# Top-k attention and a low-rank mixer on one core: a transfer queue in program order, and both heads of a pair's third step transposed by VectorE and transfers

## The chip, the core and the metric

The kernel runs on one core of a Trainium2 chip. The core has five engines that each work through their own list of instructions in order: TensorE (PE in the profile, with PEld for the loads of its stationary operand), VectorE (DVE), ScalarE (ACT), GpSimd (POOL) and SyncE (SP), which here does nothing but issue transfers. They meet through semaphores. The metric is the time of one execution on the device in microseconds, from the first to the last instruction; the kernel before takes 1765.89 us in the median of three runs (1764.58 to 1766.87).

## The reference

For 8 batches of 8 heads with 576 rows and a head size of 64, each row of scores keeps its 32 largest entries, goes through a softmax and weighs the values; then a mixer and a two-layer network run over the result.

```python
scores = scale * np.matmul(q, k.transpose(0, 1, 3, 2))          # 8 x 8 x 576 x 576
kth = np.partition(scores, -32, axis=-1)[..., -32:-31]
scores = np.where(scores >= kth, scores, -1000000000.0)
attn = np.exp(scores - np.max(scores, axis=-1, keepdims=True))
attn = attn / (np.sum(attn, axis=-1, keepdims=True) + 1e-09)
x = np.matmul(attn, v)      # then (batch, row, head*64): 8 x 576 x 512
# mixer: U (576 x 32), V (32 x 576), w_ch1 (512 x 2048), w_ch2 (2048 x 512)
h = x.transpose(0, 2, 1) @ U @ V
u = x + h.transpose(0, 2, 1)
out = u + np.maximum(u @ w_ch1, 0.0) @ w_ch2
```

## The kernel before

Two heads are worked on together as a pair; there are 32 pairs, `g`, four to a batch. A pair has five steps: in steps `t` = 0 to 3, 128 rows of both heads; in step 4 the last 64 rows of both heads together, which makes it a short step. The steps of all pairs are counted by `n`, with `g, t = divmod(n, CH)` and `CH = 5`.

In each step VectorE finds the 32 largest of every row by four rounds of "eight largest" and "replace these eight" (lines 385, 396, 400). GpSimd and ScalarE mask the scores, and ScalarE takes the exponential into `E` (line 351). To multiply `E` by the values, TensorE needs it transposed. In the early pairs TensorE transposes both heads itself, by four 128x128 transposes for each head and one for the two 64-wide remainders, and ScalarE copies the result out of PSUM into `PT`. From pair 6 on (`shared`), only head 0 goes that way; head 1 is transposed in 32x32 blocks by VectorE into `y`, and the blocks are brought into order by transfers: four writes from `y` to a DRAM tile `away`, then one read from `away` into `PT`. All of these are issued by SyncE.

```python
    def shared(g, t):
        return t < NT and g * CH + t >= ROUNDED          # ROUNDED = 30: pairs 6 to 31, NT = 4

    def blocks(g, t):
        E2 = probs[g, t]
        PT = attn.tile([P, 2 * NT + 1, P], F32, tag="PT", name="PT")
        PTs[g, t] = PT
        y = attn.tile([P, 4, NT, BLK], F32, tag="y", name="y", bufs=1)
        nc.vector.transpose(                                            # line 447
            y.rearrange("p r c j -> p c r j"),
            E2[:, S + TAIL : 2 * S].rearrange("p (c r j) -> p c r j", c=NT, r=4),
        )
        away = dram.tile([P, 4, P], F32, tag="away", name="away")
        for a in range(4):
            nc.sync.dma_start(                                          # line 453
                away[:, a].rearrange("(r i) n -> i r n", r=4),
                y[a * BLK : (a + 1) * BLK].rearrange("i r c j -> i r (c j)"),
            )
        nc.sync.dma_start(                                              # line 457
            PT[:, NT : 2 * NT].rearrange("p a n -> p (a n)"), away.rearrange("p a n -> p (a n)")
        )

    def turns(g, t):
        ...
        for h in range(1 if shared(g, t) else nh):
            tp = ps_t.tile([P, NT, P], F32, tag="tp", name="tp")
            for j in range(NT):
                a = h * (S + TAIL) + j * P
                nc.tensor.transpose(tp[:, j, :], E2[:, a : a + P], ident)   # line 475
            nc.scalar.copy(PT[:, NT * h : NT * h + NT], tp)                 # line 476
            yield
        tp = ps_t.tile([P, P], F32, tag="tp", name="tp")
        ...
        nc.tensor.transpose(tp, E2[:, a : a + P], ident)                    # line 480
        nc.scalar.copy(PT[:, NT * nh], tp)                                  # line 481
        yield

    def values(g, t):
        ...
        nc.tensor.matmul(O, lhsT=vd, rhs=PT[:, 2 * NT], start=True, stop=False)   # line 509
        PB = PT[:, NT : 2 * NT].rearrange("p a (c j) -> p c a j", c=NT) if shared(g, t) else None
        for j in range(NT):
            for h in range(2):
                nc.tensor.matmul(                                           # line 513
                    O[half(h)],
                    lhsT=va[:, h, j, :],
                    rhs=PB[:, j] if h and shared(g, t) else PT[:, NT * h + j],
                    start=False,
                    stop=(j == NT - 1),
                )
        ...
        nc.scalar.copy(XTs[g][:, cols(t)], O)                               # line 522
```

The two-layer network of a batch (`mlp`, lines 582 and 601) is 4096 matmuls over the whole kernel's 8 batches, and is cut into small portions. A call of `fill()` puts the next portion into TensorE's list; how much is fixed by counts (`share`), not by time. The order of everything in a step from pair 4 on is written out by hand:

```python
        away = n <= STEPS and shared(*divmod(n - 1, CH))
        ...
        fill()
        next(turning, None)          # transposes of step n-1 on TensorE: turns(n-1)
        fill()
        next(turning, None)
        if away:
            next(last)               # exponential of head 1 of step n-1
        fill()
        next(turning, None)
        fill()
        if ease:
            next(last, None)         # exponential of head 0 of step n-1
        if n - 2 >= ALONE:
            values(*divmod(n - 2, CH))
        if n + 1 < STEPS:
            scores(*divmod(n + 1, CH))        # lines 333, and 320 for the short step
        next(here, None)             # a round of the top-k search of step n on VectorE
        next_params(1)
        ...
        fill()
        next(here, None)
        if away:
            blocks(*divmod(n - 1, CH))
        fill()
        if n <= STEPS:
            turning = turns(*divmod(n - 1, CH))
        fill()
        next(here, None)
        ...
        fill()
```

So the block transposes of step `n-1` are made in the middle of step `n`, and its values are multiplied in the middle of step `n+1`. At the top of step 0 of each pair `load(g + 1)` brings in the next pair's inputs: 21 transfers from pair 5 on. The output of the network leaves by `turned_back`, called from within `fill()`: a transpose on TensorE (line 649), a copy on ScalarE (line 651), one or two transfers (lines 655, 660).

Before, the order of TensorE, ScalarE, VectorE and GpSimd is that of the program (`manual_schedule`); the order of SyncE's transfers is chosen by the framework's scheduler:

```python
    HT = 10       # buffers of the network's hidden layer, two 320-wide slices each
    PE, ACT = mybir.EngineType.PE, mybir.EngineType.Activation
    DVE, POOL = mybir.EngineType.DVE, mybir.EngineType.Pool
    ...
    ctx.enter_context(tc.manual_schedule(engines={PE, ACT, DVE, POOL}))
```

Of the kernel before, what the change touches and what calls it, by code (L numbers as in the profile page):

```python
# [8 lines left out]
F32 = mybir.dt.float32  # L9
# [17 lines left out]
def kernel(  # L27
# [29 lines left out]
    B, H, S, D = q.shape  # L57
    P = 128
# [4 lines left out]
    NT, TAIL = 4, 64  # L63
    MAIN = NT * P
# [5 lines left out]
    CH = NT + 1  # L70
# [3 lines left out]
    NV = 3  # L74

    BLK = 32
    HT = 10
    PE, ACT = mybir.EngineType.PE, mybir.EngineType.Activation
    DVE, POOL = mybir.EngineType.DVE, mybir.EngineType.Pool

    const = ctx.enter_context(tc.tile_pool(name="const", bufs=1))
    loads = ctx.enter_context(tc.tile_pool(name="loads", bufs=1))
    attn = ctx.enter_context(tc.tile_pool(name="attn", bufs=2))
# [3 lines left out]
    ps_s = ctx.enter_context(tc.tile_pool(name="ps_s", bufs=2, space=bass.MemoryType.PSUM))  # L87
    ps_t = ctx.enter_context(tc.tile_pool(name="ps_t", bufs=2, space=bass.MemoryType.PSUM))
    ps_m = ctx.enter_context(tc.tile_pool(name="ps_m", bufs=2, space=bass.MemoryType.PSUM))
    ctx.enter_context(tc.manual_schedule(engines={PE, ACT, DVE, POOL}))  # L90


    PARTS = ((0, 1, NT), (2, 3))
# [141 lines left out]
    probs, PTs = {}, {}  # L235
# [199 lines left out]
    def shared(g, t):  # L435


        return t < NT and g * CH + t >= ROUNDED

    def blocks(g, t):  # L440


        E2 = probs[g, t]
        PT = attn.tile([P, 2 * NT + 1, P], F32, tag="PT", name="PT")
        PTs[g, t] = PT
        y = attn.tile([P, 4, NT, BLK], F32, tag="y", name="y", bufs=1)
        nc.vector.transpose(
            y.rearrange("p r c j -> p c r j"),
            E2[:, S + TAIL : 2 * S].rearrange("p (c r j) -> p c r j", c=NT, r=4),
        )  # L450
        away = dram.tile([P, 4, P], F32, tag="away", name="away")
        for a in range(4):
            nc.sync.dma_start(
                away[:, a].rearrange("(r i) n -> i r n", r=4),
                y[a * BLK : (a + 1) * BLK].rearrange("i r c j -> i r (c j)"),
            )
        nc.sync.dma_start(
            PT[:, NT : 2 * NT].rearrange("p a n -> p (a n)"), away.rearrange("p a n -> p (a n)")
        )

    def turns(g, t):


        E2 = probs.pop((g, t))
        nh = 2 if t < NT else 1
        if shared(g, t):
            PT = PTs[g, t]
        else:
            PT = attn.tile([P, 2 * NT + 1, P], F32, tag="PT", name="PT")
            PTs[g, t] = PT  # L470
        for h in range(1 if shared(g, t) else nh):
            tp = ps_t.tile([P, NT, P], F32, tag="tp", name="tp")
            for j in range(NT):
                a = h * (S + TAIL) + j * P
                nc.tensor.transpose(tp[:, j, :], E2[:, a : a + P], ident)  # L475
            nc.scalar.copy(PT[:, NT * h : NT * h + NT], tp)  # L476
            yield
        tp = ps_t.tile([P, P], F32, tag="tp", name="tp")
        a = MAIN if nh == 2 else S - P
        nc.tensor.transpose(tp, E2[:, a : a + P], ident)  # L480
        nc.scalar.copy(PT[:, NT * nh], tp)
        yield

    def inverse(g, lo, hi):
        den = dens[g][:, lo:hi]
        if g == NPAIR - 1:
            nc.vector.tensor_scalar_add(den, den, 1e-9)
        nc.vector.reciprocal(den, den)

    def values(g, t):  # L490

        PT = PTs.pop((g, t))
        va, vd, vt = (a[g % NV] for a in (vas, vds, vts))
        O = ps_t.tile([P, P], F32, tag="tp", name="O")
        if t == NT:
            den, x = dens[g], xs[g % 2]
            inverse(g, 2 * NT if g == NPAIR - 1 else 0, 2 * NT + 1)
            for j in range(NT + 1):
                nc.tensor.matmul(  # L499
                    O,  # L500
                    lhsT=PT[:, j],
                    rhs=va[:, :, j, :] if j < NT else vt,
                    start=(j == 0),
                    stop=(j == NT),
                )
            for h in range(2):
                nc.scalar.mul(x[half(h), NT, half(h)], O[half(h), half(h)], den[half(h), 2 * NT :])
            return
        nc.tensor.matmul(O, lhsT=vd, rhs=PT[:, 2 * NT], start=True, stop=False)  # L509
        PB = PT[:, NT : 2 * NT].rearrange("p a (c j) -> p c a j", c=NT) if shared(g, t) else None  # L510
        for j in range(NT):
            for h in range(2):
                nc.tensor.matmul(  # L513
                    O[half(h)],
                    lhsT=va[:, h, j, :],
                    rhs=PB[:, j] if h and shared(g, t) else PT[:, NT * h + j],
                    start=False,
                    stop=(j == NT - 1),
                )
        if t == 0:  # L520
            XTs[g] = attn.tile([P, MAIN], F32, tag="XT", name="XT")
        nc.scalar.copy(XTs[g][:, cols(t)], O)  # L522
# [49 lines left out]
    def mlp(b):  # L572
# [3 lines left out]
        for chunks, (lo, hi) in zip(PARTS, SPAN):  # L576
            w = hi - lo
            hTs = []
            for f in range(NF):
# [11 lines left out]
                if f % 2 == 0:  # L591
                    hT = mlpp.tile([P, 2, WIDE], F32, tag="hT", name="hT", bufs=HT)
                    hTs += [hT[:, 0], hT[:, 1]]
# [102 lines left out]
    t = 0  # L696
# [5 lines left out]
    for n in range(STEPS + 2):  # L702
        g, t = divmod(n, CH)
        if n < STEPS:
            if t == 0 and g + 1 < NP:
                load(g + 1)
            if t == 1 and g + 1 < NP:
                ready = prep(g + 1)
            fronts[n] = front(g, t)
            next(fronts[n])  # L710
        here, last = fronts.get(n, iter(())), fronts.pop(n - 1, iter(()))
        if n >= ALONE - 1 and n <= ALONE:

            if n < ALONE:
                next(last)
                values(*divmod(n - 3, CH))
                list(turning)
                next(here)
                next(last)
                scores(*divmod(n + 1, CH))  # L720
                values(*divmod(n - 2, CH))
            list(turns(*divmod(n - 1, CH)))
            values(*divmod(n - 1, CH))
            if n < ALONE:
                next(here)
                next(here)
                inverse(g, 0, 2 * NT)
                mixing.append(mixed(g, 1))
                fill()
                next(here)  # L730
                continue
            fill()
            scores(*divmod(n + 1, CH))
            next(here)
            while mixing:
# [3 lines that stand above are left out]
            next(last, None)  # L739
            next(here)  # L740
            fill()
            next(here)
            next(here)
            fill()
            continue
        ease = eased(*divmod(n - 1, CH))
        if n < ALONE:
            if ease:
                next(last, None)
            scores(*divmod(n + 1, CH))  # L750
            if n >= 3:
                values(*divmod(n - 3, CH))
                if (n - 3) % CH == NT:
                    mixing.append(mixed((n - 3) // CH, 3))
            list(turning)
            fill()
            next(here)
            if t < NT:
                next_params(1)
            fill()  # L760
            next(ready, None)
            next(here)
            next(last, None)
            fill()
            next(here)
            if t in (0, 1):
                next_params(1)
            next(here)
            fill()
            if n >= 1:  # L770
                turning = turns(*divmod(n - 1, CH))
            continue
        away = n <= STEPS and shared(*divmod(n - 1, CH))
        if ease:
            next(last, None)
# [5 lines that stand above are left out]
            next(last)  # L781
# [4 lines that stand above are left out]
            next(last, None)  # L786
# [3 lines that stand above are left out]
            scores(*divmod(n + 1, CH))  # L790
        next(here, None)
        next_params(1)
        if n - 2 >= ALONE and (n - 2) % CH == NT:
            mixing.append(mixed((n - 2) // CH, 5))
        fill()
        next(here, None)
        if away:
            blocks(*divmod(n - 1, CH))
        fill()
        if n <= STEPS:  # L800
            turning = turns(*divmod(n - 1, CH))
        fill()
        next(here, None)
        next(ready, None)
        if t in (1, 3):
# [3 lines that stand above are left out]
# [33 lines left out]
```

## Time and profile before

| | before |
|---|---|
| time, median of 3 | 1765.89 us |
| span of the profiled execution | 1765.1 us |
| TensorE busy, matmuls | 1670.0 us (95%) |
| weight loads busy | 1259.5 us (71%) |
| VectorE busy | 1540.3 us (87%) |
| ScalarE busy | 1026.2 us (58%) |
| GpSimd busy | 846.4 us (48%) |
| transfers on SyncE's queue | 110.68 MB, 26.0% of 16 engines' span |
| transposes of `E`, line 475 | 736 in 184 groups of four |
| block transposes, line 447 | 104 |

The profile gives each engine's busy time, then the same cut into 40 equal slices of 44.1 us, one digit each (9 means 90% or more). It follows back the chain of work that ended last, and lists groups of instructions with count, busy time, mean duration of one and the idle time before them. Besides this page there are answers of the trace: a table of busy times over chosen windows, and a timeline of each engine with start, length, line and, in brackets, the idle time before an instruction and what ended it. A run of equal instructions is one row of the timeline, so its length reaches from the start of the first to the end of the last.

### The profile page before, as it was taken

The page shows a single profiled execution, that of the slowest core. Times are in us where ns is not written, and L with a number is a line of the kernel's source. Part 1 is how long each engine was busy: PE and PEld are TensorE (multiplying, and loading weights), DVE is VectorE, ACT ScalarE, POOL GpSimd, SP SyncE. Part 2 cuts the span into 40 slices and gives each one's busy share as a digit, 9 for nine tenths or more (in the row PEclk, how much of TensorE's full clock was granted, in tenths as well). Part 3 has the DMA queues.
Part 4 walks back from the last instruction along what each step waited for, and adds up shares of the span by engine and source line. Part 5 has one row for each costly group of instructions (what it writes and reads, how often), then busy time and mean ns, then how long its engine had stood idle before and what let it go on. Part 6 is the DMA issues. An engine that isn't in the chain of part 4 may idle for free.

```text
span 1765.1 us, 28989 instructions
## 1 busy us (share of the span) xinstructions
PE 1670.0 (95%) x9851; PEld 1259.5 (71%) x9851; DVE 1540.3 (87%) x3106; ACT 1026.2 (58%) x2682; POOL 846.4 (48%) x591
## 2 busy tenths in 40 slices
PE   4576889999999999999999999999999999999999
PEld 2444556777777877788777877788777877788677
DVE  7999989999999999999999999999999999994000
ACT  4778787655655665565656556565656656564100
POOL 4777677445545454444444454545354554543000
PEclk7677799999999999999999999999999999999999
DMA  3232232232223332222223232223233232211010
GB/s 99 84 90 72 81 85 61 51 66 70 66 59 76 72 72 64 67 66 66 61 62 81 66 72 63 70 61 70 58 68 80 64 76 56 56 45 45 4 15 13
DMA packets 275829, 112.79 MB, mean 64 GB/s; under 512 B 173920, under 2 KB 260192, under 8 KB 275680
## 3 DMA queue, kind: packets, MB, share of 16 engines
q1 hardware_dynamic: 274624, 110.68, 26.0%
q8 instruction: 77, 1.26, 0.3%
q14 instruction: 72, 0.59, 0.1%
q10 hardware_dynamic: 1056, 0.26, 0.1%
HBM read 74.15 MB, written 36.70 MB: 63 GB/s over the span
## 4 chain that ended last, share of the span: by engine, by line
PE 78%; DVE 13%; POOL 4%; ACT 3%; issue 1%; DMA 1%; SPq 0%; POOLq 0%; DVEq 0%
PE mm L582 26%; PE mm L601 25%; PE sc L333 7%; PE O L513 6%; DVE rr L396 6%; DVE m L400 5%; PE tp L475 3%; DVE first L385 2%; PE sc L320 2%; PE O L499 2%; PE up L557 1%; PE O L509 1%; POOL E L403 1%; PE up L559 1%; PE tp L649 1%
## 5 line engine op out<-in xcount | busy, mean ns | idle before, releaser
L400 DVE MAX8 m<-rr 128x8 f32<-128x576 f32 x864 | 614.3, 747 | 5.5
L601 PE MATMUL mm<-hT,w 128*128 128x256 f32 (+1 forms) x2048 | 547.4, 410 | 0.0
L582 PE MATMUL mm<-uT,w 128*128 128x256 f32 (+1 forms) x2048 | 541.1, 410 | 0.8 <-ACT hT L594 0.8
L403 POOL TENSOR_SCALAR E<-Ssb,m 128x576 f32<-128x576 f32 x127 | 280.9, 2212 | 366.2 <-DVE m L400 346.1
L582 PEld LDWEIGHTS mm<-uT,w 128*128 128x128 f32 x2048 | 371.7, 190 | 114.7 <-issue 26.0
L601 PEld LDWEIGHTS mm<-hT,w 128*128 128x128 f32 x2048 | 368.5, 190 | 106.6 <-issue 22.5
L396 DVE MATCH_REPLACE8 rr<-m,rr 128x576 f32<-128x576 f32 x576 | 423.2, 741 | 0.0
L422 POOL TENSOR_TENSOR Ssb<-Ssb,E 128x576 f32<-128x576 f32 x159 | 224.8, 1414 | 147.6 <-ACT E L421 147.6
L594 ACT ACTIVATE hT<-mm 128x320 f32<-128x320 f32 (+1 forms) x256 | 105.0, 410 | 243.8 <-PE mm L582 243.3
L351 ACT ACTIVATE E<-Ssb,nmax 128x576 f32<-128x576 f32 x288 | 223.0, 776 | 37.3 <-POOL Ssb L404 28.1
L385 DVE MAX8 first<-Ssb 128x8 f32<-128x576 f32 x288 | 203.7, 743 | 38.5 <-ACT Ssb L346 37.8
L396 DVE MATCH_REPLACE8 rr<-first,Ssb 128x576 f32<-128x576 f32 x288 | 211.7, 742 | 0.0
L404 POOL TENSOR_TENSOR Ssb<-Ssb,E 128x576 f32<-128x576 f32 x127 | 179.1, 1410 | 10.6
L333 PE MATMUL sc<-qkT 64*128 64x288 f32 x1024 | 170.7, 454 | 6.3 <-ACT Ssb L344 5.2
L513 PE MATMUL O<-PT,va 128*64 128x128 f32 x2048 | 145.4, 285 | 2.0 <-DMA PT<-away 2.0
L475 PE MATMUL tp<-ident,E 128*128 128x128 f32 x736 | 116.0, 284 | 31.5 <-ACT XT L522 11.6
L476 ACT COPY PT<-tp 128x512 f32<-128x512 f32 x184 | 106.4, 585 | 58.0 <-PE tp L475 55.4
L475 PEld LDWEIGHTS tp<-ident,E 128*128 128x128 f32 x736 | 92.5, 146 | 63.2 <-ACT XT L522 13.4
L513 PEld LDWEIGHTS O<-PT,va 128*64 128x64 f32 x2048 | 113.6, 140 | 18.5 <-DMA PT<-away 2.2
L421 ACT ACTIVATE E<-Ssb,least 128x576 f32<-128x576 f32 x159 | 123.3, 776 | 5.2
L333 PEld LDWEIGHTS sc<-qkT 64*128 64x128 f32 x1024 | 93.2, 197 | 44.6 <-issue 14.0
L614 DVE TENSOR_TENSOR oT<-uT,mm 128x320 f32<-128x320 f32 (+1 forms) x8 | 3.6, 454 | 137.1 <-PE mm L601 137.1
(81 smaller groups left out, 1576.4 us busy)
## 6 DMA issues: line engine op xcount, KB each, us to landing
away<-y SPq DMA_DIRECT2D x416, 64.0 KB, 1.8
PT<-away SPq DMA_DIRECT2D x104, 256.0 KB, 2.7
raw<-in_moe_w_ch_dram SPq DMA_DIRECT2D x32, 512.0 KB, 3.8
va<-in_v_dram SPq DMA_DIRECT2D x64, 128.0 KB, 2.2
out_dram<-ob SPq DMA_DIRECT2D x57, 128.0 KB, 2.1
ld<-in_q_dram SPq DMA_DIRECT2D x108, 64.0 KB, 2.4
ld<-in_k_dram SPq DMA_DIRECT2D x108, 64.0 KB, 2.3
ld<-in_q_dram SPq DMA_DIRECT2D x108, 8.0 KB, 2.1
```

What stands on the lines that cost most here:

```text
L333: nc.tensor.matmul(sc[:, h, 0:HALF], lhsT=qkT[half(h), 0, cols(t)], rhs=qkT[half(h), 1, i * HALF : (i + 1) * HALF], start=True, stop=True,)
L351: nc.scalar.activation(E, chunk, AF.Exp, bias=nmax, scale=SCALE, accum_out=total)
L385: nc.vector.max(ms[c], curs[c])
L396: nc.vector.match_replace(nxt, ms[c], curs[c], NEG)
L400: nc.vector.max(ms[c], curs[c])
L403: nc.gpsimd.tensor_scalar(Es[c], chunks[c], ms[c][:, 7:8], NEG, ALU.is_lt, ALU.mult)
L404: nc.gpsimd.tensor_tensor(chunks[c], chunks[c], Es[c], ALU.add)
L422: nc.gpsimd.tensor_tensor(chunks[c], chunks[c], Es[c], ALU.subtract)
L475: nc.tensor.transpose(tp[:, j, :], E2[:, a : a + P], ident)
L513: nc.tensor.matmul(O[half(h)], lhsT=va[:, h, j, :], rhs=PB[:, j] if h and shared(g, t) else PT[:, NT * h + j], start=False, stop=(j == NT ...
L582: nc.tensor.matmul(ph[:, 0:w], lhsT=w1[:, cc, f * P : (f + 1) * P], rhs=uT[:, cc, lo:hi], start=(cc == 0), stop=(cc == NC - 1),)
L601: nc.tensor.matmul(po[:, 0:w], lhsT=w2[:, f, c * P : (c + 1) * P], rhs=hTs[f][:, 0:w], start=(f == 0), stop=(f == NF - 1),)
```

## The change

In the third step of a pair (`t` = 2), from pair 6 on, head 0 is taken off TensorE too: `blocks` is called for head 1 and then for head 0, and `turns` leaves only the remainder's transpose. The purpose is to relieve TensorE of four transposes, and ScalarE of a copy, in one step of five. For two sets of blocks in flight `y` gets two buffers; to make room the hidden layer gets nine buffers in place of ten. And SyncE joins the engines whose order is that of the program, so that the transfers are issued in the order in which the code names them.

```diff
-    HT = 10
+    HT = 9
...
-    ctx.enter_context(tc.manual_schedule(engines={PE, ACT, DVE, POOL}))
+    ctx.enter_context(tc.manual_schedule(engines={PE, ACT, DVE, POOL, SP}))
...
+    def both(g, t):
+        return t == 2 and shared(g, t)
+
-    def blocks(g, t):
+    def blocks(g, t, h):
         E2 = probs[g, t]
-        PT = attn.tile([P, 2 * NT + 1, P], F32, tag="PT", name="PT")
-        PTs[g, t] = PT
-        y = attn.tile([P, 4, NT, BLK], F32, tag="y", name="y", bufs=1)
+        if h:
+            PTs[g, t] = attn.tile([P, 2 * NT + 1, P], F32, tag="PT", name="PT")
+        PT, lo = PTs[g, t], h * (S + TAIL)
+        y = attn.tile([P, 4, NT, BLK], F32, tag="y", name="y")
         nc.vector.transpose(
             y.rearrange("p r c j -> p c r j"),
-            E2[:, S + TAIL : 2 * S].rearrange("p (c r j) -> p c r j", c=NT, r=4),
+            E2[:, lo : lo + MAIN].rearrange("p (c r j) -> p c r j", c=NT, r=4),
         )
...
-            PT[:, NT : 2 * NT].rearrange("p a n -> p (a n)"), away.rearrange("p a n -> p (a n)")
+            PT[:, NT * h : NT * h + NT].rearrange("p a n -> p (a n)"), away.rearrange("p a n -> p (a n)")
...
-        for h in range(1 if shared(g, t) else nh):
+        for h in range(0 if both(g, t) else 1 if shared(g, t) else nh):
...
-        PB = PT[:, NT : 2 * NT].rearrange("p a (c j) -> p c a j", c=NT) if shared(g, t) else None
+        swapped = both(g, t), shared(g, t)
...
-                    rhs=PB[:, j] if h and shared(g, t) else PT[:, NT * h + j],
+                    rhs=(
+                        PT[:, NT * h : NT * h + NT].rearrange("p a (c j) -> p c a j", c=NT)[:, j]
+                        if swapped[h]
+                        else PT[:, NT * h + j]
+                    ),
...
         if away:
-            blocks(*divmod(n - 1, CH))
+            blocks(*divmod(n - 1, CH), 1)
+            if both(*divmod(n - 1, CH)):
+                blocks(*divmod(n - 1, CH), 0)
```

## The prediction

> **What bounds the kernel now.** I read the page first: busy shares, the 40 slices, the chain that ended last.
>
> ```profile
> PE 1670.0 (95%) x9851; PEld 1259.5 (71%) x9851; DVE 1540.3 (87%) x3106; ACT 1026.2 (58%) x2682; POOL 846.4 (48%) x591
> PE   4576889999999999999999999999999999999999
> DVE  7999989999999999999999999999999999994000
> PE 78%; DVE 13%; POOL 4%; ACT 3%; issue 1%; DMA 1%; SPq 0%; POOLq 0%; DVEq 0%
> ```
>
> Three stages show. In the first six slices VectorE is nearly full and TensorE is not. In a long middle both digits are 9. In the last three slices VectorE has nothing left and TensorE finishes the last batch's network alone. The chain puts 78% on TensorE. Who leads in the middle is read from busy times by windows:
>
> ```profile
> core 0: us, PE busy (x) PEld busy (x) DVE busy (x) ACT busy (x) POOL busy (x), PEclk, DMA share, GB/s
> 900.00:1000.00 100.00, 100.00 (x614) 76.97 (x612) 96.21 (x193) 59.39 (x162) 48.21 (x32) 1.00 0.30 68
> ```
>
> TensorE has no gap; VectorE idles about 4 us in 100. The timeline repeats itself every 200.1 us, which is four pairs, so a pair lasts 50.0 us. TensorE sets this pace, with VectorE 2 us per pair behind it in load. Therefore whatever makes TensorE wait in the middle is lost time, since its list is in order and has no slack to win it back.
>
> Next, one third step and the start of the short step after it: VectorE, SyncE, then TensorE.
>
> ```profile
> 998.80 0.69 DVE L447 STREAM_TRANSPOSE y<-E 128x512 f32<-128x512 f32 x1
> ```
> ```profile
> 999.52 1.76 SPq L453 DMA_DIRECT2D away<-y  x4
> ...
> 1002.80 0.34 SPq L457 DMA_DIRECT2D PT<-away  x1
> ```
> ```profile
> 1004.58 0.60 PE L475 MATMUL tp<-ident,E 128*128 128x128 f32 x4
> 1005.01 1.03 PE L601 MATMUL mm<-hT,w 128*128 128x256 f32 x4
> ...
> 1007.17 1.09 PE L513 MATMUL O<-PT,va 128*64 128x128 f32 x16
> ```
>
> Head 1's transpose ends at 999.49. Four writes go out, the read is issued at 1002.80, and at 1007.17 TensorE uses the result. The page gives 2.7 us from the read's issue to its landing, so it is there at about 1005.5, some 1.7 us early. This margin is what the change draws on.
>
> [...] SyncE issues the read 3.28 us after the first write (999.52 to 1002.80), when the last write, issued at about 1000.84, has landed (1.8 us on the page). [...] Here 100.00 against 76.97; I rely on the absence of gaps and on starts, not on the 100.
>
> **The change part by part.** It touches pairs 6 to 31: 26 third steps.
>
> *TensorE loses four transposes per pair.* The group's mean of one is 284 ns, four would be 1.14 us, but they overlap. What they occupy in the list is the distance of starts: 1004.58 to 1005.01 = 0.43 us. In sum 26 x 0.43 = 11.2 us.
>
> *ScalarE loses a copy* of 585 ns per pair; at 59% it is not on the path: 0.
>
> *VectorE gains a transpose:*
>
> ```profile
> L447 DVE STREAM_TRANSPOSE y<-E 128x512 f32<-128x512 f32 x104 | 72.6, 698 | 21.0 <-ACT E L351 19.9
> ```
>
> 26 x 0.70 = 18.1 us. Per pair 0.7 us of the about 2 us that VectorE idles: it fits. Head 0's exponential ends about 1.1 us before the end of head 1's transpose in this pair, and up to 0.8 us after it in others; then VectorE waits a little, still within its slack.
>
> *SyncE gains five transfers per pair, in the program's order:* four writes for head 1, its read, four writes for head 0, its read. With T the end of head 1's transpose:
> - Head 1's read is issued at T + 3.3 (1002.80 - 999.49; the undisturbed steps show 3.2 to 3.3).
> - It takes 0.34 us to issue. Head 0's transpose has long been done by then, but its first write stood behind the read: it starts at T + 3.66.
> - The same set of writes again, 3.24 us: head 0's read is issued at T + 6.90.
> - From a read's issue to a waiting TensorE the trace has one direct example, just after the shared pairs begin:
>
> ```profile
> 356.47 0.39 SPq L457 DMA_DIRECT2D PT<-away  x1
> ```
> ```profile
> 359.36 1.09 PE L513 MATMUL O<-PT,va 128*64 128x128 f32 x14 [1.98 <-DMA PT<-away]
> ```
>
> That is 2.89 us. So head 0's part can be used at T + 9.79.
>
> When does TensorE want it? The four pairs of a period have the first L513 of this step at T + 8.11, 7.68, 8.15 and 6.98: mean 7.73. With the transposes gone TensorE gets there 0.43 earlier: T + 7.30. It waits 9.79 - 7.30 = 2.49 us, and against the old schedule it is 9.79 - 7.73 = **2.06 us later per pair**. The wait can't be overlapped: the rest of the network's matmuls stand behind L513 in the list, and head 0's first block is the first thing that L513 multiplies.
>
> Does T move away from under this? VectorE starts step 3's search when its scores arrive, about 2.1 us after TensorE makes them (at 989.83; the search starts at 991.91), and the transpose lies 6.9 us into that search. If TensorE is late by 2 us, the next pair's scores are late by the same, VectorE idles more at the start of it, and the offsets return. The loss repeats in each pair: 26 x 2.06 = 53.6 us. In the first one or two of these pairs VectorE was still behind (T + 4.92 and 5.67); I add 1 us for that.
>
> *The order of the other transfers.* A pair's 21 loads come as a block at step 0: 16 x 0.62 + 5 x 0.53 = 12.6 us of SyncE. Step 0 has no write to `away` behind it until step 1, where the transpose ends some 16 us after the last read of the pair before was issued, so they fit. An output that precedes the writes in the program can hold them until ScalarE has copied it; I find one place per four pairs where that is so (a transpose L649 at 1041.32 right after the scores of step 3), worth 0.2 us or so. In the first stage the weight loads hold the queue in both orders: 0, plus or minus 4 us.
>
> *Nine hidden buffers:* a half of the network uses eight at a time, and the ninth lets the next half begin; the tenth is not missed, because the oldest are read first. 0.
>
> Sum: 1765.9 + 53.6 + 1 = 1820.5, rounded to **1820 us**, slower by 3.1%.
>
> **The rivals.**
> - *The transfers are hidden and TensorE's relief counts.* Then -11.2 us: 1755. For it: 95% of TensorE, and the trip is hidden today. Against it: the margin is 1.7 us or less, while a second round trip in the same queue costs 6.5 us more.
> - *VectorE becomes the bound.* At most +18.1 us if none of the added time fits: 1784. For it: 96% in the middle. Against: idle of 2 us per pair, just at the short step that follows.
> - *Queueing order alone.* Outputs or loads ahead of the `away` writes make steps 0, 1 and 3 late too. Their reads have margins of 2 to 4 us today. If half of the pairs lost 1 us more, 13 us on top: 1833. The reverse is open too: today's order puts loads among the writes (3.28 us for four at 1007.99), and program order takes that away, but no wait hangs on it.
> - *The second trip is shorter than I think,* if writes overlap the read before them better. Each 0.5 us less is 13 us.
>
> **Range and chances.** The one term that matters is 2.06 us per pair. With 1.3 to 2.8 us it gives 34 to 73 us; the start adds a few. Range 1798 to 1838. The limit of 2% is at 1801.2, which needs 1.36 us per pair. Faster by over 2% has no path from a relief of 11 us: 0.03. Within 2%: 0.16. Slower: 0.81.
>
> **What would show it.** Right: TensorE gains an idle time ahead of L513, put down to the read `PT<-away`, about 2.5 us in each pair, 60 to 65 us in all; a pair lasts about 52 us; VectorE's share in the middle falls to about 94% although it does more; SyncE's second set of writes starts about 3.7 us after the end of head 1's transpose. Wrong: no such idle time, or TensorE's gaps put down to VectorE or ScalarE; the line counts (632 for L475, 130 transposes) with the old 50 us per pair. What would make it wrong: a second trip that lands before T + 7.3, or a T that runs ahead of TensorE.

## The result, and the profile after

The changed kernel takes 1868.54 us in the median of four runs (1865.06 to 1872.74), against 1766.38 us of the kernel before beside it: a ratio of 1.058, 95% interval 1.056 to 1.061. It is 102 us slower. The prediction had 1820 us, with a range of 1798 to 1838: the direction was right, the size was not. About half of the loss was in the sum; the rest is a longer round trip than I had reckoned, and the clock of TensorE, which I had left out altogether.

The page after, same views as before: busy shares, slices (with the granted clock), the chain that ended last.

```profile
PE 1686.0 (90%) x9747; PEld 1263.6 (68%) x9747; DVE 1557.7 (83%) x3132; ACT 1015.6 (54%) x2656; POOL 846.2 (45%) x591
PE   4655889889999998999999999999999999999999
DVE  7999998899898988999889889899889989985000
PEclk7788999899999999999999999999999999999999
PE 47%; DVE 31%; DMA 8%; ACT 4%; POOL 4%; SPq 3%; issue 3%; DVEq 0%; POOLq 0%
```

TensorE and VectorE both lose share in the middle. The windows view gives it, the first line from before, the second from after (columns: window, its length, then busy time and count of TensorE, of its weight loads, of VectorE, ScalarE and GpSimd, the granted clock of TensorE, the share of the transfer engines, GB/s):

```profile
400.00:1600.00 1200.00, 1197.90 (x7296) 914.28 (x7294) 1149.63 (x2309) 717.74 (x1923) 575.60 (x384) 1.00 0.28 66
400.00:1600.00 1200.00, 1131.44 (x6647) 854.54 (x6645) 1082.11 (x2163) 655.22 (x1753) 536.05 (x359) 0.97 0.31 72
```

TensorE falls from 99.8% to 94.3%, VectorE from 95.8% to 90.2%. The chain says what came between: TensorE falls from 78% to 47%, transfers rise from 1% to 8% and SyncE's queue from 0 to 3%. The chain now runs round a ring, from VectorE over the transfers to TensorE and back. A somewhat longer middle of the changed kernel, which the later runs are compared on:

```profile
400.00:1700.00 1300.00, 1227.20 (x7232) 928.19 (x7231) 1171.29 (x2345) 710.52 (x1905) 578.42 (x387) 0.97 0.30 72
```

TensorE is without work for 5.6% of it, and its granted clock, 1.00 before, is 0.97. The group of the value multiplication carries the idle time (before, then after):

```profile
L513 PE MATMUL O<-PT,va 128*64 128x128 f32 x2048 | 145.4, 285 | 2.0 <-DMA PT<-away 2.0
L518 PE MATMUL O<-PT,va 128*64 128x128 f32 x2048 | 151.5, 293 | 79.5 <-DMA PT<-away 79.5
```

The 2.0 us of before become 79.5 us in 26 waits, one per pair, in the third step's values and nowhere else. One of them in the timeline; SyncE first:

```profile
1104.29 1.76 SPq L458 DMA_DIRECT2D away<-y  x4
1107.51 0.34 SPq L462 DMA_DIRECT2D PT<-away  x1
1107.89 1.88 SPq L458 DMA_DIRECT2D away<-y  x4
1111.50 0.34 SPq L462 DMA_DIRECT2D PT<-away  x1
```

Two round trips stand one behind the other: head 1's four writes and its read, then head 0's. Head 0's block transpose was over at 1105.20, but SyncE issues nothing from 1106.05 to 1107.51, and head 0's first write starts behind the read, at 1107.89. TensorE in the same stretch:

```profile
1111.69 0.38 PE L514 MATMUL O<-PT,vd 128*128 128x128 f32 x2
1114.18 1.09 PE L518 MATMUL O<-PT,va 128*64 128x128 f32 x16 [2.11 <-DMA PT<-away]
1115.21 2.15 PE L333 MATMUL sc<-qkT 64*128 64x288 f32 x8
1117.29 3.70 PE L591 MATMUL mm<-uT,w 128*128 128x320 f32 x10
```

It stands for 2.11 us until the read has landed. Then comes something that the prediction doesn't have: the eight score matmuls take 2.08 us from their start to the next instruction, and one step later, from 1125.40 to 1126.57, they take 1.17 us:

```profile
1125.40 1.24 PE L333 MATMUL sc<-qkT 64*128 64x288 f32 x8
1126.57 4.58 PE L591 MATMUL mm<-uT,w 128*128 128x320 f32 x16
```

The clock goes with it, in windows of 4 us:

```profile
1116.00:1120.00 4.00, 4.00 (x13) 2.33 (x12) 1.87 (x4) 2.65 (x7) 0.00 (x0) 0.65 0.41 94
1120.00:1124.00 4.00, 4.00 (x19) 2.92 (x18) 4.00 (x10) 1.66 (x5) 1.40 (x1) 1.00 0.38 60
```

The seventh number, the granted clock, is 0.65 after the wait and 1.00 again 4 us later.

### The profile page after: what moved, and what is told of

It reads as the page before. It is cut to its first block, busy times and chain, and to the rows that moved or that the text cites. A ratio compares the mean times of both kernels' runs of the same rounds, so it can differ in the third digit from the quotient of the medians.

```text
span 1867.0 us, 28942 instructions
## 1 busy us (share of the span) xinstructions
PE 1686.0 (90%) x9747; PEld 1263.6 (68%) x9747; DVE 1557.7 (83%) x3132; ACT 1015.6 (54%) x2656; POOL 846.2 (45%) x591
## 4 chain that ended last, share of the span: by engine, by line
PE 47%; DVE 31%; DMA 8%; ACT 4%; POOL 4%; SPq 3%; issue 3%; DVEq 0%; POOLq 0%
PE mm L610 19%; DVE rr L396 12%; DVE m L400 11%; PE mm L591 11%; PE sc L333 6%; DVE first L385 4%; PE O L518 4%; DMA away<-y 4%; DMA PT<-away 4%; DVE y L452 2%; SPq L458 2%; PE tp L480 2%; POOL E L403 1%; PE O L504 1%; ACT E L351 1%
## 5 line engine op out<-in xcount | busy, mean ns | idle before, releaser
L591 PEld LDWEIGHTS mm<-uT,w 128*128 128x128 f32 x2048 | 375.6, 192 | 122.5 <-issue 30.6
L610 PEld LDWEIGHTS mm<-hT,w 128*128 128x128 f32 x2048 | 372.6, 192 | 112.4 <-issue 25.8
L518 PE MATMUL O<-PT,va 128*64 128x128 f32 x2048 | 151.5, 293 | 79.5 <-DMA PT<-away 79.5
L333 PE MATMUL sc<-qkT 64*128 64x288 f32 x1024 | 186.8, 490 | 8.8 <-ACT Ssb L344 7.8
L518 PEld LDWEIGHTS O<-PT,va 128*64 128x64 f32 x2048 | 118.2, 144 | 97.2 <-DMA PT<-away 84.4
L333 PEld LDWEIGHTS sc<-qkT 64*128 64x128 f32 x1024 | 101.0, 214 | 52.1 <-issue 17.8
L480 PE MATMUL tp<-ident,E 128*128 128x128 f32 x632 | 99.0, 282 | 37.1 <-ACT XT L531 15.6
L480 PEld LDWEIGHTS tp<-ident,E 128*128 128x128 f32 x632 | 78.0, 144 | 64.2 <-ACT XT L531 17.5
L481 ACT COPY PT<-tp 128x512 f32<-128x512 f32 x158 | 91.7, 586 | 52.5 <-PE tp L480 50.0
```

The lines of the kernel that those rows point to most:

```text
L333: nc.tensor.matmul(sc[:, h, 0:HALF], lhsT=qkT[half(h), 0, cols(t)], rhs=qkT[half(h), 1, i * HALF : (i + 1) * HALF], start=True, stop=True,)
L518: nc.tensor.matmul(O[half(h)], lhsT=va[:, h, j, :], rhs=(PT[:, NT * h : NT * h + NT].rearrange("p a (c j) -> p c a j", c=NT)[:, j] if swap ...
L591: nc.tensor.matmul(ph[:, 0:w], lhsT=w1[:, cc, f * P : (f + 1) * P], rhs=uT[:, cc, lo:hi], start=(cc == 0), stop=(cc == NC - 1),)
L610: nc.tensor.matmul(po[:, 0:w], lhsT=w2[:, f, c * P : (c + 1) * P], rhs=hTs[f][:, 0:w], start=(f == 0), stop=(f == NF - 1),)
```

## The experiments

Throughout, T is the end of head 1's block transpose in the third step, and "T + x" the start of the value multiplication L518 that needs both heads. The mean over the 26 pairs is T + 7.57 before and T + 10.32 in the changed kernel.

**Program order alone.** Nothing but the order of SyncE's list and the buffer counts changes.

```diff
     def both(g, t):
-        return t == 2 and shared(g, t)
+        return False
```

> Only the transfer queue's order is that of the program (with two buffers of y and nine of the hidden layer); in the third step head 0 stays on TensorE as before. Theory (the wait for head 0's second round trip, and what follows from it, makes all of the +102 us): 1766 us, within 6 us. Rival (the program's order lets loads and outputs stand ahead of the writes): a good part of the 102 us, 1790 us or more, with waits of TensorE for PT<-away also in steps 0, 1 and 3.

Measured: 1765.58 us, ratio 0.9996 (0.9987 to 1.0004). The program's order and the ninth buffer cost nothing, as the theory had it; the rival falls.

**The scheduler's order with both heads.**

```diff
-    ctx.enter_context(tc.manual_schedule(engines={PE, ACT, DVE, POOL, SP}))
+    ctx.enter_context(tc.manual_schedule(engines={PE, ACT, DVE, POOL}))
```

> The changed kernel, but with SyncE's order left to the scheduler as before. Theory (round trips in series): the wait in the third step's values stays, about 3 us per pair or more because loads come between; 1860 to 1890 us. Rival (the program's order is the cause): 1760 to 1790 us.

Measured: 1918.47 us, ratio 1.086 (1.085 to 1.088). The rival is wrong in sign: the program's order does not cause the loss, it saves 50 us of it. My range was too low as well. SyncE's timeline in one third step shows why:

```profile
1076.62 3.24 SPq L458 DMA_DIRECT2D away<-y  x7
1080.11 0.34 SPq L462 DMA_DIRECT2D PT<-away  x1
1080.49 5.60 SPq L458 DMA_DIRECT2D away<-y  x4
1086.26 0.34 SPq L462 DMA_DIRECT2D PT<-away  x1
```

By the counts, three of head 0's writes go ahead of head 1's read, which is good; but then head 0's last write is followed by three writes of the next step, whose transpose is not yet made. The group of four takes 5.60 us, and head 0's read stands behind it. It is issued at T + 9.5 or later in half of the pairs, the values start at T + 11.69 in the mean, and 116 us of waits result.

**The transfers made, but not used.** In the third step TensorE transposes and uses head 0 as before; the blocks and the five transfers are made too and land in a tile of their own.

```diff
-    HT = 9
+    HT = 8
...
-            PT[:, NT * h : NT * h + NT].rearrange("p a n -> p (a n)"), away...
+            to.rearrange("p a n -> p (a n)"), away...      # to: PT for head 1, a scratch tile for head 0
-        for h in range(0 if both(g, t) else 1 if shared(g, t) else nh):
+        for h in range(1 if shared(g, t) else nh):
-        swapped = both(g, t), shared(g, t)
+        swapped = False, shared(g, t)
```

> Head 0's block transpose and its five transfers are made in the third step, in the changed kernel's order, but land in a tile that nobody reads; TensorE keeps its own transposes and multiplies what they give. The eighth hidden buffer pair is given up for the room. Theory (it is the waiting for the second round trip): no wait of TensorE for PT<-away in step 4, 1766 to 1772 us. Rival (VectorE's added 18 us, or the load on the transfer engines and SyncE): 1785 us or more.

Measured: 1767.92 us, ratio 1.0008 (1.0000 to 1.0017). VectorE's 26 transposes more, SyncE's 130 transfers more and 13.65 MB more on the transfer engines (126.44 against 112.79) together cost 2 us (0 to 3 by the interval). So the loss is in the waiting for head 0, not in the work.

**Useless work in the wait, too much of it.** Eight matmuls are put ahead of the third step's values.

```diff
+        if both(g, t):
+            dm = ps_t.tile([P, 512], F32, tag="tp", name="dm")
+            for _ in range(8):
+                nc.tensor.matmul(dm[:, 0:320], lhsT=ident, rhs=V[:, 0:320], start=True, stop=True)
         O = ps_t.tile([P, P], F32, tag="tp", name="O")
```

> The changed kernel with eight matmuls of 320 columns of no use (2.2 us) put ahead of the third step's values, in the place where TensorE waits. Output unchanged. Theory (a wait of over 2 us costs its length and then some 1.3 us more, because the granted clock falls to 0.65 after it): the idle time shrinks from 3.1 to about 1 us per pair, the clock in the middle stays at 0.99 to 1.00, and the time falls by 26 x 1.3 = 34 us to about 1835 us. Rival (the clock's fall is not due to the idle time, or costs nothing): 1865 to 1875 us, since the matmuls only fill a wait.

Measured: 1869.33 us, ratio 1.059 (1.057 to 1.061). By the number this is the rival's result, but the timeline says that the test was not the one I meant:

```profile
1111.21 4.47 PE L502 MATMUL dm<-V,ident 128*128 128x320 f32 x16
```

Each of the eight runs as two instructions, and they fill 4.3 us, more than the wait. The values came at T + 11.57 instead of T + 10.32, so that the kernel took the same time with a later start of the values and a clock of 1.00. That is in favour of the theory, but it had to be tried with the right length.

**Half of it.** Four matmuls, 2.2 us.

```diff
-            for _ in range(8):
+            for _ in range(4):
```

> The last try's useless matmuls ran as two passes each and took 4.3 us, longer than the wait. Here four of them, 2.2 us, ahead of the third step's values. Theory (the fall of the granted clock after a wait costs extra): some 0.9 us of idle time stays per pair, the clock in the middle is 0.99 to 1.00, and the time falls by the clock's part, some 26 x 1.3 = 34 us, to 1830 to 1840 us. Rival (the clock's fall costs nothing, the loop over VectorE and the transfers sets the pace): 1863 to 1873 us.

Measured: 1844.78 us, ratio 1.045 (1.043 to 1.047). Work that nobody uses makes the kernel 24 us faster. The values start no earlier than in the changed kernel (T + 10.45), the waits shrink from 79 to 31 us, and the clock is back; the same middle as above:

```profile
400.00:1700.00 1300.00, 1271.85 (x7555) 965.74 (x7554) 1178.11 (x2360) 718.92 (x1928) 586.93 (x393) 1.00 0.30 73
```

So the fall of the clock after the wait cost about 24 us of the 102. The 34 us that I expected were too many: in some pairs the wait is not followed by a slow clock.

**Both heads' writes first, then both reads.**

```diff
-        nc.sync.dma_start(
+        return lambda: nc.sync.dma_start(
             PT[:, NT * h : NT * h + NT].rearrange("p a n -> p (a n)"), away.rearrange("p a n -> p (a n)")
         )
...
-            blocks(*divmod(n - 1, CH), 1)
+            reads = [blocks(*divmod(n - 1, CH), 1)]
             if both(*divmod(n - 1, CH)):
-                blocks(*divmod(n - 1, CH), 0)
+                reads.append(blocks(*divmod(n - 1, CH), 0))
+            for read in reads:
+                read()
```

> The changed kernel, with the eight writes of both heads issued first and then the two reads, so that the second round trip runs beside the first. Theory (two round trips in series in one queue): head 0's read is issued at about T + 5.5 instead of T + 7.3 (T is the end of head 1's block transpose), usable at T + 8.4; TensorE waits about 1.1 us per pair, 1780 to 1800 us. Rival (the wait is set by the transfer engines' speed, not by SyncE's standing): the same 1868 us.

Measured: 1791.87 us, ratio 1.014 (1.013 to 1.016), in the middle of the expected range, and the values start at T + 8.43 in the mean. The transfers themselves are the same. What cost 77 us of the 102, the clock's part included, is that SyncE stood at head 1's read while head 0's writes were ready behind it.

**Both heads in the first step instead of the third.**

```diff
-        return t == 2 and shared(g, t)
+        return t == 0 and shared(g, t)
```

> The changed kernel, with both heads going by transfers in the first step of a pair instead of the third. There TensorE wanted the values at T + 10.6 to 11.6 in the kernel before, against T + 7.0 to 8.2 in the third step. Theory (arrival at T + 10 against the moment of need): hardly any wait, TensorE's relief of 11 us counts: 1753 to 1768 us. Rival (two sets of blocks in one queue are too much wherever they are): 1800 us or more.

Measured: 1769.42 us, ratio 1.0016 (1.0009 to 1.0022), just above the range. The large loss is gone, as the theory had it: two serial trips fit where TensorE asks later. The gain is missing. In the steady part four pairs take 199.2 us instead of 200.1, half of the 1.7 us that four times 0.43 would give; and at the first scores of pair 9 (462.7 us) the kernel is 5.6 us behind the run with program order alone (457.1). From 300 to 470 us TensorE waits 5.1 us for the reads, against 1.5 us in that run; what else holds it in those first pairs I did not settle.

**The third step's values late.**

```diff
+        tardy = n - 2 >= ALONE and both(*divmod(n - 2, CH))
-        if n - 2 >= ALONE:
+        if n - 2 >= ALONE and not tardy:
             values(*divmod(n - 2, CH))
...
         next(here, None)
         fill()
+        if tardy:
+            values(*divmod(n - 2, CH))
```

> The changed kernel, with the third step's values taken behind the next scores and three portions of the network, at the end of the short step. Transfers and transposes are the same. Theory (the wait is one of place in TensorE's list): the values now come at about T + 10.9, the wait is gone or under 0.5 us, VectorE gets its scores early again, and 1753 to 1770 us follows. Rival (VectorE's 18 us or SyncE become the bound once the wait is gone): 1780 us or more.

Measured: 1764.66 us, ratio 0.9990 (0.9983 to 0.9997). The same transposes and the same serial trips, only asked for at T + 11.01 instead of being waited for: 104 us of difference. The pair lasts 49.8 us. VectorE carries its added work without becoming the bound:

```profile
400.00:1600.00 1200.00, 1195.27 (x7210) 904.39 (x7205) 1167.17 (x2337) 700.95 (x1899) 575.63 (x385) 1.00 0.33 77
```

**Late values and writes first.** The edits of "both heads' writes first" and of "values late" together; that the late values are those of a third step is now written out.

```diff
+        tardy = n - 2 >= ALONE and (n - 2) % CH == 2 and both(*divmod(n - 2, CH))     # values at the end of the step
...
+            reads = [blocks(*divmod(n - 1, CH), 1)]                                    # reads behind both heads' writes
```

> The values of the third step late (as in the run before) and, besides, both heads' writes issued ahead of both reads. With the values late alone, six waits for PT<-away of 4 us in all were left in the middle, and a pair lasted 49.8 us instead of 50.0. Theory (the round trip is the only thing that holds): these waits go, 0.17 us per pair more, 1758 to 1764 us. Rival (VectorE at 97% is the bound by now): 1764 to 1767 us.

Measured: 1760.06 us, ratio 0.9966 (0.9953 to 0.9978). TensorE's waits for the reads fall from 4.4 to 1.8 us over the whole run, and the time by 4.6 us, within the expected range; the waits alone make 2.6 us of it.

**The same from pair 9 on.**

```diff
-        return t == 2 and shared(g, t)
+        return t == 2 and shared(g, t) and g >= 9
```

> As the one before, but both heads go by transfers from pair 9 on only, because in pairs 6 to 8 VectorE comes late to its block transposes (12.5 us after the scores instead of 9.7), so that its added 0.7 us is not hidden there. Theory (VectorE is behind in the first pairs and catches up): 2 to 3 us less than the run before, 1756 to 1762 us. Rival (it makes no difference where it starts): the same as the run before, or 0.6 us more for three pairs' relief given up.

Measured: 1762.67 us, ratio 0.9981 (0.9974 to 0.9989). A miss: it is slower by 2.6 us, not faster. The start is not what loses: the first scores of pair 7 come at 359.1 us here and at 354.6 us where pair 6 already has its values late, but those of pair 10 at 503.8 against 504.1 us. The profiled execution falls 1.7 us behind between pairs 16 and 17, where TensorE waits once for a read, 1.46 us up to 847.0 us; the run before has no such wait there. Why it comes I did not settle.

**Two steps of five.**

```diff
-        return t == 2 and shared(g, t) and g >= 9
+        return t in (0, 2) and shared(g, t) and g >= 9
```

The values stay late in the third step only.

> As the one before, and both heads by transfers in the first step of a pair too, which relieves TensorE of 0.43 us per pair once more and gives VectorE 0.7 us. Theory of TensorE as the bound: 5 us less again, about 1753 us. Rival (VectorE is full: 48.0 us of work per pair in the kernel before, 49.4 with two transposes more, of 49.8): no gain, or up to 10 us more, 1760 to 1770 us.

Measured: 1756.02 us, ratio 0.9942 (0.9928 to 0.9955), 6.7 us below the run before it, where 5 were expected. This is the fastest of all, 10 us faster than the kernel before. VectorE is at 98.5% in the middle and still not the bound, and TensorE hardly waits:

```profile
400.00:1600.00 1200.00, 1194.36 (x7159) 902.90 (x7158) 1181.60 (x2367) 695.76 (x1887) 580.55 (x388) 1.00 0.37 87
```

## Why the prediction was right and wrong

**Right: who waits for what.** TensorE waits ahead of L518 for `PT<-away`, once per pair, in the third step alone (3.06 us in the mean, where 2.49 were forecast); a pair lasts 53.7 us (about 52 forecast); 632 transposes and 130 block transposes as counted; VectorE's and SyncE's added work is hidden (2 us where it is made without being used); program order and the ninth buffer cost nothing. And the wait is not won back. The kernels whose clock stays at 1.00 in the middle lie within 4 us of one line: 26 times the delay of the third step's values against T + 7.57 of before.

| kernel | values at T + | 26 x delay, us | measured loss, us | clock, 400 to 1700 us |
|---|---|---|---|---|
| writes first | 8.43 | 22.4 | 25.7 | 1.00 |
| useless work, half | 10.45 | 74.8 | 78.6 | 1.00 |
| useless work, whole | 11.57 | 103.9 | 103.2 | 1.00 |
| the change | 10.32 | 71.6 | 102.2 | 0.97 |
| scheduler's order | 11.69 | 107.0 | 152.3 | 0.95 |

**Wrong, first step: the size of the delay, "2.06 us later per pair".** It is 2.75 us. The prediction had head 1's read at T + 3.3, head 0's read at T + 6.90, the values at T + 9.79. The medians are 3.24, 7.26 and 9.99, so the second trip, "the same set of writes again, 3.24 us", is the mis-sized term: from its first write to its read it takes 3.61 us in the median. Its four writes are issued in 1.87 us instead of 1.76, while head 1's read is under way, and its read follows the issue of the last write by 2.17 us instead of 1.86. The means lie higher still, at 3.52, 7.57 and 10.32: in 7 of the 26 pairs already head 1's read is issued later than T + 3.5. I took undisturbed trips for the mean of all. In the early pairs TensorE had asked sooner: with them the mean of before is T + 7.57 and not 7.73, worth 4 us where the sum had added 1. This makes 71.6 us in place of the predicted 54.6.

**Wrong, second step: "it waits 2.49 us" was taken for all that the wait costs.** No term stood for the clock. The last column of the table shows it: the two kernels in which TensorE stands idle longest lie 31 and 45 us above their line, and they are the two whose mean clock falls. The traces agree in size: from 340 us on, the clock stands at one half for 25 stretches of 3.41 us in the changed kernel, in which TensorE is busy for 76.9 us, and for 38 of them with 99.9 us in the scheduler's order. Half of these busy times, 38 and 50 us, is the most that the clock can have cost, by an estimate in which work at half the clock takes twice as long (the score matmuls above took 2.08 us instead of 1.17). Filling the wait with useless matmuls took 24 us off, with the values no earlier. The example was even on show in the prediction: the kernel before has one wait of 1.98 us, and the score matmuls behind it (360.38 in its timeline) took 2.29 us instead of 1.24. I used that row for the latency of the read and left the row behind it out of account.

Together 71.6 and 24 make 95.6 of the 102 us. As the useless work delayed the values by another 0.12 us per pair, 26 x 0.12 = 3 us, the clock's share is more like 27 us. The remaining 4 us I leave open.

**Wrong, third: the rival "-11.2 us" was dismissed for the right reason, but its size too was too large.** With hardly any wait left (1.8 us), the relief in one step of five gives 6 us (late values, writes first), not 11.

## What to carry to other kernels

Before work is moved from a full engine to a chain of transfers, ask when the result is wanted and count the chain as it will stand in the queue: here SyncE, standing for 1.46 us at head 1's read, held head 0's writes, which were ready behind it, so issue everything that is ready first, and then the dependent reads (77 us of the 102). In a loop in which one engine is full, place the consumer later in that engine's list rather than hope for the margin; here the same transfers cost 102 us or nothing, depending on where one step's value multiplication stood. And when TensorE gets a repeated wait, reckon the wait and the slow stretch that may come after it: here 19 of 25 waits, all of 1.89 us or more, had one.

## What the hardware showed that I had not expected

Behind a wait of about 2 us TensorE's granted clock could be 0.50, as in the second line of the view below, but it was not so behind every one. In the changed kernel 25 of the 26 waits have score matmuls behind them. 19 of these were followed by score matmuls at about half speed (1.7 to 2.2 us instead of 1.17); the shortest such wait was 1.89 us, and the longest without a slow stretch 3.17 us. In the kernel with the writes first, 20 waits of 0.2 to 1.9 us had no slow stretch behind them.

The trace of the changed kernel shows where the difference lies. Every stretch at full or at half clock in it, but for the last, which ends with the run, lasts 3.41 us or a multiple of that (51.20 and 102.40 us are the most frequent at full clock), and the idle time of TensorE within one window of this grid went with the clock of the next. Here are two waits of nearly the same length, 2.11 us (ended at 1114.18) and 2.17 us (ended at 1222.57), in windows cut at the grid:

```profile
1111.99:1115.40 3.41, 1.30 (x19) 1.04 (x20) 2.17 (x4) 1.02 (x4) 0.55 (x1) 1.00 0.56 149
1115.40:1118.81 3.41, 3.41 (x11) 2.00 (x10) 0.68 (x2) 1.68 (x6) 0.00 (x0) 0.50 0.40 99
1217.80:1221.22 3.42, 2.59 (x14) 2.09 (x12) 3.14 (x7) 1.76 (x6) 3.34 (x3) 1.00 0.46 130
1221.22:1224.63 3.41, 2.06 (x24) 1.54 (x24) 2.15 (x4) 1.58 (x5) 0.40 (x1) 1.00 0.54 149
1224.63:1228.04 3.41, 3.41 (x19) 2.90 (x18) 2.37 (x6) 2.32 (x9) 0.00 (x0) 1.00 0.22 77
```

The first wait lies in one window, TensorE works for 1.30 of its 3.41 us, and the next window has half the clock. The second is cut in two by the grid, 0.83 and 1.35 us, and the clock stays at 1.00. In this trace, from 340 to 1720 us, 17 windows at full clock had over 2.0 us of idle time, and each was followed by one at half clock; of 356 with less than 1.7 us none was; of the six in between, 1.76 to 2.00 us, three were. In the kernel before, the one window with more than 1.7 us, 1.98 us of idle time, was followed by one at half clock, and none of the 401 others was. No run was made to test this apart; it is read off these two traces.
